# A new order for the opening of an H3 and MLP training step: v loaded in place, two filter spectra kept on chip, tap rows filled to 128

## The chip, the cores and the metric

The kernel runs on one core of a Trainium2 chip. The metric is the time of one execution in device microseconds (us), as the median of several executions. The core has five instruction queues that work side by side: TensorE (PE, matrix products; its weight loads are listed as PEld), VectorE (DVE), ScalarE (ACT), GpSimd (POOL) and SyncE (SP, which only issues transfers). POOL issues transfers too, on a queue of its own. Each queue runs its instructions strictly in the order in which they stand; an instruction whose input is not there holds up everything behind it in its queue.

## The reference

A token sequence of 2048 by 512 goes through four layers, A B A B, each of the form x = x + f(layernorm(x)); the kernel returns the output and all gradients for a given grad_out. Cut to what matters here:

```
def _A_ref(q, k, v, shift_k, ssm_k, ssm_D):          # q is layernorm(x)
    k_shift = sum over t<4 of k[:, s-t, :] * shift_k[:, t]   # short causal filter
    kv = k_shift * v
    y = irfft(rfft(pad(kv)) * rfft(pad(ssm_k)))[:S]  # long causal convolution, per column
    return q * (y + kv * ssm_D)
def _B_ref(x, w1, b1, w2, b2):                        # gelu MLP, 512 -> 1376 -> 512
    return gelu(x @ w1 + b1) @ w2 + b2
```

The long convolution does not depend on x, so kv, its spectrum, the filter's spectrum H and y are computed once, for both A layers.

## The kernel before, in words

The program has four stages: the opening, the forward convolution, the MLP with both B layers, and the backward pass. The change is in the opening and at its seam to the forward convolution.

**The opening** (function `opening`) makes, from the raw inputs, four things. First the filter: the rows of ssm_k ("hat", four loads into the memory that later holds the MLP weights, `res.w`, `w_sb` in the views) are turned by TensorE against an identity (`both`), with a reversed copy made by DVE (`hrev`), into a folded form X (`fold_x`), from which DVE makes the sums and differences `fold_s`, `fold_d`, `fold_t`. Second the sine and cosine tables `tabN` and `tabF`: POOL writes step numbers (`krow`), DVE multiplies them and masks them to a phase (`tab_u`, `tab_ph`), ACT takes the sine. Third k and v: k (`kn`) is turned into `kT`, the four-tap filter is 16 products with diagonal matrices (`wdiag`) for each of 16 token tiles (the "ks" steps, results in `ksb`), v's second half is mirrored by TensorE (the "mv" steps) and written back over v and to DRAM (`vB_d`), and DVE multiplies `ksb` by v into `kv` (`y_res` in the views). Fourth q: mirrored likewise ("mq"), its layernorm statistics taken and applied, and stored (`n_d`).

Then come 16 spectrum steps "H", in five groups `GROUPS` of 2, 2, 4, 4, 4: each is 4 or 8 matmuls of 128x512 of the folded filter with `tabN` into a PSUM tile `sp_ps`, plus one or two matmuls of 5 rows (`sp5` against `hsp`) that add five single taps, 31 of these in all. Each step is copied to SBUF (`Hg`, two slots for pairs of steps) and stored in DRAM (`Hspec_d`). Between these steps TensorE transposes the tables (steps "tt").

The order of all this is not written by hand. Each step is entered into a list (`Plan`) with an engine, an estimated duration, and what it reads and writes; `Plan.order` takes the steps by earliest start and a priority from the table `OPEN_W`; `OPEN_EV` says by a letter which engine copies each PSUM tile (A for ACT, V for DVE). The result is fixed for every queue.

**The forward convolution** (function `phase_conv_forward`) takes the five groups in turn: spectrum of kv (`spectrum`, into `KVg`), product with H on DVE (`product`: `pr_t`, `pr_u`, `Yg`), inverse transform on TensorE (`inv_group`, PSUM tile `iv_ps`). H comes from DRAM by `load_spec`, two buffers `Hg2` in rotation; groups 0 and 1 are loaded right behind the opening. Ten small matmuls (`keep_busy`, on `nyq`) stand ahead of the first inverse transform.

Of the kernel before, what the change touches and what calls it, by code (L numbers as in the profile page):

```python
# [178 lines left out]
SIN_SCALE = -(2.0 * math.pi / 8192.0) * (1.0 - SIN_EPS)  # L179
# [176 lines left out]
class InvBlocks:  # L356
# [45 lines left out]
OPEN_SLOTS = {"sp": 3, "p1": 2, "kn": 4, "hg": 2, "vt": 2, "kb": 2, "ft": 2, "ph": 2}  # L402
OPEN_EV = {"hx": "AVAAAAAV", "kt": "AAAVVAVV", "ks": "AAAAAAAAVAAAAAAA", "mv": "VAAV", "mq": "AAAA", "H": "AAAAAAAAAAAAAAVA"}
OPEN_W = {
    "PE": {1: -302, 3: 4, 4: -70, 6: 29, 7: 0},
    "ACT": {1: -63, 3: -115, 4: -256, 5: 338, 6: 142, 7: 164},
    "DVE": {1: -17, 2: -176, 3: -9, 4: 62, 5: 0, 8: 60},
    "POOL": {3: 197, 4: 117, 5: 0, 7: 78, 8: -90},
    "SP": {0: -7, 4: 29, 6: -224},
}  # L410
OPEN_FREE = {"PE": 4.2, "ACT": 3.3, "DVE": 3.8, "POOL": 8.4, "SP": 0.7}

# [4 lines left out]

def opening(nc, tc, dims, consts, dram, res, aps, tabFs, foldp, iop, hrot, gp, psum):
# [15 lines left out]
    wdiag = gp.tile([P, ND, 4, P], BF16, name="wdiag")  # L434
    krow = gp.tile([P, 1280], I32, name="krow")

# [41 lines left out]
    p = Plan(OPEN_SLOTS)  # L478
    line = {"ks": [], "H": []}

# [16 lines left out]
    def four(t):  # L497
        return t[:, :].rearrange("p (t d) -> p t d", t=4)
# [13 lines left out]
    for cc in (1, 0, 3, 2):  # L512
# [9 lines left out]
        for m in (1, 0):  # L522
            ps = ("sp", "hx", cc, m)
# [13 lines left out]
    S_(0.5, lambda b: b.nc.sync.dma_start(out=wsh, in_=aps["A_shift_k"].rearrange("(c p) j -> p c j", p=P)), 0,  # L537
       writes=[("wsh",)])
    S_(0.5, lambda b: b.nc.sync.dma_start(out=hsp[4:5, :], in_=aps["A_ssm_D"].rearrange("(o d) -> o d", o=1)), 0,
       part=[("hsp",)])  # L540

    def hs(b):
# [48 lines left out]
    def wd(b):  # L591
        for c in range(ND):
            for j in range(4):
                b.nc.vector.tensor_scalar(out=wdiag[:, c, j, :], in0=consts.ident, scalar1=wshf[:, c, j:j + 1], scalar2=None,
                                          op0=ALU.mult)
    wshf = gp.tile([P, ND, 4], F32, name="wsh_f")
    V(0.08, lambda b: b.nc.vector.tensor_copy(out=wshf, in_=wsh), 3, reads=[("wsh",)], writes=[("wshf",)])
    V(1.7, wd, 3, reads=[("wshf",)], writes=[("wd",)])
    G(0.6, lambda b: b.nc.gpsimd.dma_start(out=dram.wdiag, in_=wdiag), 3, reads=[("wd",)], kb=512.0)

# [141 lines left out]
    for g, (k1, base, n) in enumerate(GROUPS):  # L742
        key = f"h{k1}"
        for mt in range(n):
            ps, hg = ("sp", "H", g, mt), ("hg", g, mt // 2)
            need = [("tN", f, qt, int(base >= 8)) for f in range(2) for qt in range(2)] + ([("tNs", int(base >= 8))] if mt >= 2 else [])
            more = 2 if g == 0 and mt == 0 else 0

            def mm(b, g=g, mt=mt, ps=ps, key=key, k1=k1, base=base):
# [19 lines left out]
            line["H"] = [E(0.215 * (6 if k1 in (0, 4) else 10) + 0.215 * more, mm, 6, after=line["H"], writes=[ps],  # L769
                           reads=need + [("ft", key), ("sp5",), ("hsp",), ("altq",)] + ([("fd",)] if k1 == 2 else []))]  # L770
            evict(OPEN_EV["H"][base + mt], lambda b, hg=hg, mt=mt: b(hg)[:, :].rearrange("p (c m d) -> p c m d", c=2, m=2)[:, :, mt % 2, :],
                  lambda b, ps=ps: b(ps), 1, 6, reads=[ps], part=[hg])
            if mt % 2:
                S_(0.45, lambda b, hg=hg, c=base + mt - 1: b.nc.sync.dma_start(
                    out=dram.Hspec[:, :, c:c + 2, :], in_=b(hg)[:, :].rearrange("p (c m d) -> p c m d", c=2, m=2)), 6,
                   reads=[hg], kb=512.0)
# [58 lines left out]
    G(1.0, ends, 8)  # L835
    return p, tiles, stk, fk, tabI_name


@with_exitstack
def phase_conv_forward(ctx, nc, tc, dims, consts, dram, res, aps):  # L840
# [29 lines left out]
    p, tiles, stk, fk, tabI_name = opening(nc, tc, dims, consts, dram, res, aps, tabFs, foldp, iop, hrot, gp, psum)  # L870
    order = p.order(open_prio, lambda o: 0.0, dict(OPEN_FREE))
# [42 lines left out]
    for g, (k1, base, n) in enumerate(GROUPS):  # L914
# [304 lines left out]
def tok(ap2d, s):  # L1219
    return ap2d[s * 512:(s + 1) * 512, :].rearrange("(t p) d -> p t d", p=P)  # L1220
# [931 lines left out]
```

## Time and profile before

| | |
|---|---|
| median of 3 runs | 828.21 us (823.02 to 828.89) |
| the profiled execution | 826.01 us, span of its instructions 824.2 us |
| PE, DVE, ACT, POOL busy, of the span | 94%, 87%, 71%, 26% |
| opening, by the queues | about 0 to 96 us of the span |
| forward convolution, TensorE's part | about 96 to 156 us |

All times in the views count from the start of the span. Matmuls overlap in the array, so a group's busy time is longer than the distance between starts; for TensorE's pace the starts are read. A number in square brackets at the end of a timeline row is the idle time of that engine before the row, with what ended it. "issue" in the chain is time that the profile can't put down to anything. In the windows the granted TensorE clock is 1.00 for 2.4 GHz and 0.50 for 1.2 GHz. A DMA share of 1.00 means that the core's 16 DMA engines were all busy.

### The profile page before, as it was taken

The numbers are of one execution on the slowest core, as the hardware profiler recorded it, in microseconds if no ns is written. First come the engines' busy times: TensorE is split into PE (matmuls) and PEld (weight loads), VectorE is DVE, ScalarE is ACT, GpSimd is POOL, SyncE is SP. The second block draws the span as 40 slices with busy tenths as digits, with TensorE's granted clock in tenths as the row PEclk, the third lists the DMA queues.
The fourth block names the chain that finished last, engine by engine and source line by source line (L and its number), as shares of the span: only waits on it lengthen the run. The fifth ranks groups of instructions, "written<-read, shape, count | busy, mean of one in ns | idle before, by whom it ended". The sixth has DMA issues, their size and how long they took to land.

```text
span 824.2 us, 14206 instructions
## 1 busy us (share of the span) xinstructions
PE 771.1 (94%) x5312; PEld 465.6 (56%) x5312; DVE 713.4 (87%) x1273; ACT 581.9 (71%) x828; POOL 213.5 (26%) x329
## 2 busy tenths in 40 slices
PE   6889879998999999999999999998999999999997
PEld 5654334565666666667566566643444456856663
DVE  7979499898999999999889998797399999993873
ACT  5777645679999999998779966425323238797663
POOL 3725200021334343235323223330111404400000
PEclk9999979999999999999999999999999999999999
DMA  8786969524565645957858477989699999883311
GB/s 263 241 320 232 331 216 326 180 53 138 165 179 137 188 122 148 239 144 202 209 166 195 116 224 203 289 217 259 186 291 276 250 380 320 259 295 100 109 59 44
DMA packets 203211, 170.46 MB, mean 207 GB/s; under 512 B 94403, under 2 KB 180614, under 8 KB 202886
## 3 DMA queue, kind: packets, MB, share of 16 engines
q1 hardware_dynamic: 189046, 125.21, 54.3%
q0 software_dynamic: 13040, 42.25, 14.6%
q10 hardware_dynamic: 1056, 2.10, 0.7%
q8 instruction: 41, 0.67, 0.4%
q14 instruction: 28, 0.23, 0.1%
HBM read 77.41 MB, written 76.36 MB: 187 GB/s over the span
## 4 chain that ended last, share of the span: by engine, by line
PE 38%; DVE 34%; ACT 15%; issue 6%; DMA 4%; POOL 3%; ACTq 0%; SPq 0%; DVEq 0%; POOLq 0%
PE sp_ps L56 10%; ACT l_g L56 9%; DVE l_g L56 8%; PE dw_ps L56 7%; PE oo_ps L56 5%; PE mm_ps L56 4%; PE iv_ps L56 4%; PE gh_ps L56 3%; DVE Wb L56 3%; DVE l_h L56 2%; DVE b_junk L56 2%; PE p_ps L56 2%; PE gk_ps L56 2%; DVE pr_u L56 2%; PE dw_tp L56 1%
## 5 line engine op out<-in xcount | busy, mean ns | idle before, releaser
L56 ACT ACTIVATE l_g<-l_g 128x1536 bf16<-128x1536 bf16 (+1 forms) x96 | 134.4, 1431 | 1.3 <-DVE l_g L56 1.1
L56 PEld LDWEIGHTS <-l_h 128*128 128x128 bf16 x704 | 69.1, 98 | 81.5 <-DVE l_h L56 3.5
L56 PEld LDWEIGHTS <-dw_tm 128*128 128x128 bf16 x704 | 66.1, 98 | 68.3 <-ACT dw_tm L1845 0.8
L56 PEld LDWEIGHTS <-w_sb 128*128 128x128 bf16 x872 | 82.5, 98 | 34.6 <-issue 11.8
L56 PE MATMUL mm_ps<-l_nT,w_sb 128*128 128x256 bf16 x704 | 89.7, 273 | 1.0 <-ACT l_g L56 0.6
L56 PE MATMUL oo_ps<-w_sb,l_h 128*128 128x512 bf16 x352 | 82.7, 384 | 3.0 <-DVE l_h L56 2.7
L56 PE MATMUL dw_ps<-x_sl,dw_tm 128*128 128x512 bf16 x352 | 85.5, 380 | 0.0
L56 PE MATMUL dw_ps<-G,dw_tm 128*128 128x512 bf16 x352 | 84.8, 379 | 0.3 <-ACT dw_tm L1845 0.3
L56 PE MATMUL mm_ps<-l_nT,w2T_sb 128*128 128x256 bf16 x704 | 82.9, 273 | 1.3 <-ACT l_h L56 0.9
L56 PE MATMUL oo_ps<-w1T_sb,l_h 128*128 128x512 bf16 x352 | 79.1, 379 | 0.1
L56 PEld LDWEIGHTS <-w2T_sb 128*128 128x128 bf16 x704 | 68.9, 98 | 14.2 <-issue 2.1
L56 DVE TENSOR_TENSOR l_g<-l_g,l_g 128x1280 bf16<-128x1280 bf16 (+1 forms) x88 | 76.6, 883 | 0.3
L56 ACT ACTIVATE l_h<-mm_ps 128x512 bf16<-128x512 f32 (+1 forms) x96 | 51.9, 594 | 28.0 <-PE mm_ps L56 19.0
L1845 ACT ACTIVATE dw_tm<-dw_tp 128x1024 bf16<-128x1024 bf16 x44 | 44.9, 1023 | 19.9 <-PE dw_tp L56 19.5
L56 POOL TENSOR_SCALAR l_dg<-ident,b_cols 128x128 bf16<-128x128 bf16 x32 | 31.6, 987 | 75.5 <-DVE b_junk L56 72.2
L56 POOL TENSOR_SCALAR rstd<-ln_mvs 128x2 f32<-128x2 f32 x20 | 13.3, 663 | 107.3 <-DVE ln_mvs L56 107.1
L1923 ACT ACTIVATE dw_o<-dw_ps 128x512 bf16<-128x512 f32 x22 | 13.1, 595 | 38.3 <-PE dw_ps L56 29.2
L56 ACT ACTIVATE l_n<-x_sl,nmr,rstd 128x512 bf16<-128x512 bf16 x48 | 37.9, 845 | 2.8 <-POOL nmr L56 1.6
L56 ACT ACTIVATE l_g<-mm_ps,b_col 128x256 bf16<-128x256 f32 x77 | 32.6, 531 | 5.4 <-PE mm_ps L56 5.2
L56 DVE TENSOR_SCALAR l_g<-l_g 128x1536 bf16<-128x1536 bf16 (+1 forms) x64 | 32.5, 519 | 2.5 <-ACT l_g L56 2.5
L56 DVE TENSOR_REDUCE b1a<-dw_fm 128x1 f32<-128x2048 bf16 x14 | 31.5, 2278 | 1.5 <-DMA dw_fm<-gz_d 1.5
L56 ACT ACTIVATE l_n<-l_n,b_cols 128x512 bf16<-128x512 bf16 x32 | 25.4, 844 | 10.2 <-POOL b_cols L56 10.1
(316 smaller groups left out, 1656.7 us busy)
## 6 DMA issues: line engine op xcount, KB each, us to landing
h_d<-l_h SPq DMA_DIRECT2D x16, 704.0 KB
gz_d<-l_h SPq DMA_DIRECT2D x16, 704.0 KB
dw_fm<-gz_d SPq DMA_DIRECT2D x22, 512.0 KB
l_n<-n_d SPq DMA_DIRECT2D x28, 256.0 KB
n_d<-l_n SPq DMA_DIRECT2D x24, 256.0 KB
Hspec_d<-Hg SPq DMA_DIRECT2D x8, 512.0 KB
Hg<-Hspec_d SPq DMA_DIRECT2D x3, 1024.0 KB
KVspec_d<-KVg SPq DMA_DIRECT2D x3, 1024.0 KB
```

The costliest lines, as they stand in the source:

```text
L56: return self.tc.keep_in_program_order(f(*args, **kwargs))
L1845: nc.scalar.activation(out=dst, in_=ps, func=ACT.Identity)
L1923: nc.scalar.activation(out=o, in_=ps, func=ACT.Identity)
```

## The change

- **v in place.** The four loads of v go into the memory of `kv` itself. They no longer wait for a slot of `vt`. The product with `ksb` then overwrites v, so it comes after the store of v's mirrored half to `vB_d` has read it.
- **Two spectra kept.** A tile `Hkeep` holds groups 0 and 1 of H from the opening on; they are still stored for the backward pass, but no longer loaded for the forward one. Group 2 is loaded behind the opening, group 3 into `Hkeep` after the product of group 1, group 4 into the one `Hg2` that is left.
- **Tap rows filled to 128.** `hsp` and `sp5` get 128 rows of which 123 are zero (two memsets on DVE at the front), so the 31 tap matmuls have 128 rows. They, and `krow` (now 16-bit), live in unused ends of `res.w`.
- **Tap masks held back.** The two DVE masks `tap_ph` may enter the list only from 9 us of its clock on.
- The 16 multiplications that make `wdiag` become one with a broadcast operand; the letters in `OPEN_EV` move two copies of v and one of k from DVE to ACT and one of q and one of ks the other way (those of hx and H only change places); 22 instead of 20 matmuls on the identity at the start; new numbers in `OPEN_W`, and so another order on every queue.

```diff
-OPEN_EV = {"hx": "AVAAAAAV", "kt": "AAAVVAVV", "ks": "AAAAAAAAVAAAAAAA", "mv": "VAAV", "mq": "AAAA", "H": "AAAAAAAAAAAAAAVA"}
+OPEN_EV = {"hx": "AAVAAAAV", "kt": "AAAAVVAV", "ks": "AAAAAAAVAAAVAAAA", "mv": "AAAA", "mq": "AVAA", "H": "AVAAAAAAAAAAAAAA"}
 OPEN_W = {
-    "PE": {1: -302, 3: 4, 4: -70, 6: 29, 7: 0},
+    "PE": {1: -464, 3: 11, 4: 31, 6: 37, 7: 7},
...
-    krow = gp.tile([P, 1280], I32, name="krow")
+    krow = res.w.flat[0][:, 2 * S + 16:2 * S + 16 + 1280].bitcast(I16)
-    hsp = gp.tile([5, D], BF16, name="hsp")
+    hsp = res.w.centre
-    sp5 = gp.tile([5, 2, 5 * P], BF16, name="sp5")
+    sp5 = res.w.flat[1][:, 2 * S + 16:2 * S + 16 + 1280].rearrange("p (f q) -> p f q", f=2)
...
+    def zero(b):
+        b.nc.vector.memset(hsp, 0.0)
+        b.nc.vector.memset(sp5, 0.0)
+    V(0.7, zero, 1, writes=[("hsp",), ("sp5",)])
...
-        V(0.48, lambda b, u=u: ...bitwise_and), 1, writes=[nm])
+        late.add(V(0.48, lambda b, u=u: ...bitwise_and), 1, writes=[nm]))
...
     def wd(b):
-        for c in range(ND):
-            for j in range(4):
-                b.nc.vector.tensor_scalar(out=wdiag[:, c, j, :], in0=consts.ident, scalar1=wshf[:, c, j:j + 1], ...
+        b.nc.vector.tensor_tensor(out=wdiag..., in0=consts.ident[:, :].unsqueeze(1).to_broadcast([P, 4 * ND, P]),
+                                  in1=wsh[...].unsqueeze(2).to_broadcast([P, 4 * ND, P]), op=ALU.mult)
...
     for i in range(4):
-        S_(0.45, ...dma_start(out=four(b(("vt", "v", i))), in_=tok(v_ap, i)), 0, writes=[("vt", "v", i)],
-           kb=512.0, after=prods[i - 2:i - 1] if i > 1 else ())
+        S_(0.45, ...dma_start(out=kv[:, 4 * i:4 * i + 4, :], in_=tok(v_ap, i)), 0, writes=[("v", i)], kb=512.0)
...
-        prods.append(V(1.23, prod, 3, reads=[("kb", "k", i), ("vt", "v", i)], part=[("kv",)]))
+        prods.append(V(1.23, prod, 3, reads=[("kb", "k", i), ("v", i)], writes=[("v", i)], part=[("kv",)]))
...
-            ps, hg = ("sp", "H", g, mt), ("hg", g, mt // 2)
+            ps, hg = ("sp", "H", g, mt), ("hg", g, mt // 2) if g > 1 else ("hk", g)
...
+    hkeep = iop.tile([P, 2, 4, 512], BF16, name="Hkeep")
-    for _ in range(20):
+    for _ in range(22):
...
-        Hs.append(invp.tile([P, 2, 4, 512], BF16, name="Hg2", tag="Hg2", bufs=2))
+        Hs.append(hkeep if g == 3 else invp.tile([P, 2, 4, 512], BF16, name="Hg2", tag="Hg2", bufs=1))
-    load_spec(0)
-    load_spec(1)
+    Hs += [hkeep[:, :, 0:2, :], hkeep[:, :, 2:4, :]]
+    load_spec(2)
...
-        if g + 2 < 5:
+        if 1 <= g <= 2:
             load_spec(g + 2)
```

**DVE at the start of the opening** (`hrev` is the reversed filter row, `tap_ph` the mask, `tab_u` and `tab_ph` the table phases, `fold_x` a copy of a turned filter tile). Before:

```order
L56 CAST pvh<-pvh_i 128x2
L56 TENSOR_SCALAR tap_ph<-tap_ph 5x640 x2
L56 COPY hrev<-w_sb 128x1024
L56 MEMSET hrev 128x4
L56 TENSOR_SCALAR tab_u<-krow,pvn 128x768
```

and now:

```order
L56 CAST pvh<-pvh_i 128x2
L56 MEMSET w_centre 128x256
L56 MEMSET w_sb 128x640
L56 COPY hrev<-w_sb 128x1024
L56 MEMSET hrev 128x4
L56 TENSOR_SCALAR tab_u<-w_sb,pvn 128x768
```

The two masks have left the place ahead of the first reversed row (they now stand behind the third and the fourth), and two memsets that wait for nothing have taken it.

**SP at the seam** (stores of H and of the normalized q, then the loads of H and the stores of kv's spectrum). Before:

```order
L56 DMA Hspec_d<-Hg_181 256x1x1024
L56 DMA n_d<-w_sb 128x4x512 x3
L56 DMA Hspec_d<-Hg_180 256x1x1024
L56 DMA Hg_1285<-Hspec_d 128x2x1024
L56 DMA Hg_1287<-Hspec_d 128x2x1024
L56 DMA KVspec_d<-KVg 256x1x1024
```

and now:

```order
L56 DMA n_d<-w_sb 128x4x512 x2
L56 DMA Hspec_d<-Hg_180 256x1x1024
L56 DMA n_d<-w_sb 128x4x512
L56 DMA Hg_1270<-Hspec_d 128x2x2048
L56 DMA KVspec_d<-KVg 256x1x1024 x2
```

The two loads of groups 0 and 1 behind the last store are gone; in their place stands one load, of group 2, and the last store of q now comes after the last store of H.

**POOL in the middle of the opening** (`ks_d` and `kT_d` are stores for the backward pass, `vB_d` and `qB_d` those of the mirrored halves). Before:

```order
L56 DMA qB_d<-w_sb 128x2x512
L56 DMA vB_d<-vt_182 128x2x512
L56 DMA qB_d<-w_sb 128x2x512 x3
L56 DMA vB_d<-vt_183 128x2x512
L56 DMA ks_d<-ksb_185 128x2048
L56 COPY kT<-kT 128x4x3
L56 DMA kT_d<-kT 128x8704
L56 DMA vB_d<-vt_182 128x2x512
```

and now:

```order
L56 DMA vB_d<-y_res 128x2x512
L56 COPY kT<-kT 128x4x3
L56 DMA vB_d<-y_res 128x2x512
L56 DMA kT_d<-kT 128x8704
L56 DMA ks_d<-ksb_185 128x2048
L56 DMA vB_d<-y_res 128x2x512 x2
```

All four stores of v now come ahead of those of q; the last two stand behind the store of `kT`, and each of them has to be through before DVE's product may overwrite that part of v.

## Rows read from the trace of the kernel before

**Rows 1.** Windows: stretch, length, busy PE, PEld, DVE, ACT, POOL, clock, DMA share.
```profile
8.20:94.00 85.80, 78.54 (x673) 46.79 (x674) 75.15 (x145) 63.44 (x78) 37.47 (x49) 0.98 0.77 272
```
**Rows 2.** The chain of waits at the seam: start us, us, what.
```profile
95.62 8.55 DMA Hg<-Hspec_d
...
105.45 0.17 DVE pr_t L56
...
107.95 0.61 DVE Yg L56
...
108.61 3.57 PE iv_ps L56 x8
```
**Rows 3.** Timeline of ACT at the seam: start us, us, row.
```profile
96.93 2.86 ACT L296 ACTIVATE KVg<-sp_ps 128x1024 bf16<-128x1024 f32 x3 [0.19 <-PE sp_ps L56]
```
**Rows 4.** Timeline of PE at the seam and in the forward convolution.
```profile
98.46 1.25 PE L56 MATMUL iv_ps<-nyq,ident 128*128 128x256 bf16 x10
108.61 1.86 PE L56 MATMUL iv_ps<-Yg,vt 128*128 128x512 bf16 x4 [8.89 <-DVE Yg L56]
...
119.22 1.03 PE L56 MATMUL iv_ps<-Yg,vt 128*128 128x512 bf16 x4
120.08 1.03 PE L56 MATMUL iv_ps<-Yg,ksb 128*128 128x512 bf16 x4
```
**Rows 5.** Windows at the seam, columns as in the first group.
```profile
104.00:106.00 2.00, 0.00 (x0) 0.00 (x0) 1.60 (x5) 0.00 (x0) 0.00 (x0) 0.50 0.91 351
```
**Rows 6.** Timeline of DVE at the start.
```profile
6.26 0.72 DVE L56 TENSOR_SCALAR tap_ph<-tap_ph 5x640 int32<-5x640 int32 x1 [2.11 <-POOL tap_ph L471]
7.68 0.64 DVE L56 TENSOR_SCALAR tap_ph<-tap_ph 5x640 int32<-5x640 int32 x1 [0.69 <-POOL tap_ph L471]
8.24 0.40 DVE L56 COPY hrev<-w_sb 128x1024 bf16<-128x1024 bf16 x1
8.69 0.62 DVE L56 TENSOR_SCALAR tab_u<-krow,pvn 128x768 int32<-128x768 int32 x1
```
**Rows 7.** Timeline of PE at the start.
```profile
4.47 0.39 PE L56 MATMUL sp_ps<-both,w_sb 128*128 128x256 bf16 x1 [0.36 <-DMA w_sb<-in_A_ssm_k_dram]
8.71 0.40 PE L56 MATMUL sp_ps<-both,hrev 128*128 128x256 bf16 x1 [3.84 <-DVE hrev L56]
```
**Rows 8.** Timeline of PE in one H step of ten matmuls.
```profile
69.64 0.39 PE L56 MATMUL sp_ps<-hsp,sp 5*128 5x512 bf16 x1
69.96 1.04 PE L56 MATMUL sp_ps<-fold_t,tabN 128*128 128x512 bf16 x4
70.93 0.39 PE L56 MATMUL sp_ps<-hsp,sp 5*128 5x512 bf16 x1
```
**Rows 9.** Groups of PE by shape, 38.7 to 94.2: busy us, mean ns.
```profile
L56 PE MATMUL sp_ps<-fold_t,tabN 128*128 128x512 bf16 x88 | 24.3, 381 | 0.0
L56 PE MATMUL sp_ps<-hsp,sp 5*128 5x512 bf16 x31 | 11.9, 385 | 0.0
```
**Rows 10.** Who waited for whom, PE, 8.7 to 96: us, times, longest.
```profile
PE sp_ps L56 <- DMA vt<-in_A_v_dram: 2.4, 1, 2.4
PE p_ps L56 <- ACT ksb L56: 1.4, 2, 0.7
PE sp_ps L56 <- DVE kT L56: 1.3, 1, 1.3
```
**Rows 11.** Timeline of DVE: the diagonals, a copy from PSUM, a memset.
```profile
18.09 2.69 DVE L56 TENSOR_SCALAR wdiag<-ident,wsh_f 128x128 bf16<-128x128 bf16 x16
...
53.73 1.23 DVE L56 CAST vt<-sp_ps 128x1024 bf16<-128x1024 f32 x1 [2.69 <-PE sp_ps L56]
...
126.81 0.48 DVE L56 MEMSET w_centre<- 128x512 bf16 x1 [0.17 <-DVE w_sb L56]
```
**Rows 12.** Issues of transfers before 96: count, KB each, us to landing.
```profile
kT_d<-kT POOLq DMA_DIRECT2D x1, 2176.0 KB, 9.2
...
vB_d<-vt POOLq DMA_DIRECT2D x4, 256.0 KB, 3.5
```

More of the change, by code (lines that the diff above doesn't have):

```diff
@@ L402, with opening @@
 OPEN_SLOTS = {"sp": 3, "p1": 2, "kn": 4, "hg": 2, "vt": 2, "kb": 2, "ft": 2, "ph": 2}
-OPEN_EV = {"hx": "AVAAAAAV", "kt": "AAAVVAVV", "ks": "AAAAAAAAVAAAAAAA", "mv": "VAAV", "mq": "AAAA", "H": "AAAAAAAAAAAAAAVA"}
+OPEN_EV = {"hx": "AAVAAAAV", "kt": "AAAAVVAV", "ks": "AAAAAAAVAAAVAAAA", "mv": "AAAA", "mq": "AVAA", "H": "AVAAAAAAAAAAAAAA"}
+OPEN_FREE = {"PE": 4.4, "ACT": 3.3, "DVE": 4.2, "POOL": 9.0, "SP": 0.7}
 OPEN_W = {
-    "PE": {1: -302, 3: 4, 4: -70, 6: 29, 7: 0},
[L406 to L409, printed above, removed]
+    "PE": {1: -464, 3: 11, 4: 31, 6: 37, 7: 7},
+    "ACT": {1: -441, 3: -237, 4: -358, 5: 436, 6: 201, 7: 70},
+    "DVE": {1: -333, 2: -77, 3: 151, 4: 332, 5: 112, 8: -88},
+    "POOL": {3: 335, 4: -45, 5: 22, 7: -90, 8: -305},
+    "SP": {0: 126, 4: -128, 6: -90},
 }
-OPEN_FREE = {"PE": 4.2, "ACT": 3.3, "DVE": 3.8, "POOL": 8.4, "SP": 0.7}
 def open_prio(o):
     return OPEN_W.get(o.eng, {}).get(o.stage, 0) - o.up
-def opening(nc, tc, dims, consts, dram, res, aps, tabFs, foldp, iop, hrot, gp, psum):
+def opening(nc, tc, dims, consts, dram, res, aps, tabFs, foldp, iop, hrot, gp, psum, hkeep):
     S, D, NT, ND = dims.S, dims.D, dims.NT, dims.ND
@@ L478, in opening @@
     p = Plan(OPEN_SLOTS)
-    line = {"ks": [], "H": []}
+    line, late = {"ks": [], "H": []}, set()
     def adder(eng, lat0):
@@ L538, in opening @@
        writes=[("wsh",)])
+    def zero(b):
+        b.nc.vector.memset(hsp, 0.0)
+        b.nc.vector.memset(sp5, 0.0)
+    V(0.7, zero, 1, writes=[("hsp",), ("sp5",)])
     S_(0.5, lambda b: b.nc.sync.dma_start(out=hsp[4:5, :], in_=aps["A_ssm_D"].rearrange("(o d) -> o d", o=1)), 0,
-       part=[("hsp",)])
+       reads=[("hsp",)], part=[("hspD",)])
     def hs(b):
@@ L548, in opening @@
     E(0.3, hs, 1, reads=[("hat", cc) for cc in range(4)], writes=[("p1", "hs")])
-    V(0.68, lambda b: b.nc.vector.tensor_copy(out=hsp[0:4, :], in_=b(("p1", "hs"))[0:4, :]), 1, reads=[("p1", "hs")],
-      part=[("hsp",)])
+    V(0.68, lambda b: b.nc.vector.tensor_copy(out=hsp[0:4, :], in_=b(("p1", "hs"))[0:4, :]), 1, reads=[("p1", "hs"), ("hsp",)],
+      part=[("hspD",)])
     for f, u in enumerate((sp5u, krow5)):
         nm = ("five", f)
-        V(0.48, lambda b, u=u: b.nc.vector.tensor_single_scalar(out=u, in_=u, scalar=8191, op=ALU.bitwise_and), 1, writes=[nm])
+        late.add(V(0.48, lambda b, u=u: b.nc.vector.tensor_single_scalar(out=u, in_=u, scalar=8191, op=ALU.bitwise_and), 1, writes=[nm]))
         def five(b, f=f, u=u):
-            b.nc.scalar.activation(out=sp5[:, f, :], in_=u, func=ACT.Sin, scale=SIN_SCALE, bias=consts.pibias[0:5, :])
-        A(0.81, five, 1, reads=[nm], part=[("sp5",)])
+            b.nc.scalar.activation(out=sp5[0:5, f, :], in_=u, func=ACT.Sin, scale=SIN_SCALE, bias=consts.pibias[0:5, :])
+        A(0.81, five, 1, reads=[nm, ("sp5",)], part=[("sp5r",)])
     def small(b):
-        b.nc.vector.memset(sp5[:, 1, 0:1], 1.0)
+        b.nc.vector.memset(sp5[0:5, 1, 0:1], 1.0)
         b.nc.vector.memset(altq, 0.0)
         b.nc.vector.tensor_copy(out=altq[:, 0:1], in_=consts.alt)
-    V(0.3, small, 1, writes=[("sp5",), ("altq",)])
+    V(0.3, small, 1, writes=[("sp5r",), ("altq",)])
     fold = Fold(nc, foldp, True)
@@ L569, in sums @@
         fold.open(hld["X"])
-    V(2.29, sums, 2, reads=[("hX",), ("sp5",)], writes=[("fs",)])
+    V(2.29, sums, 2, reads=[("hX",), ("sp5r",)], writes=[("fs",)])
     def stream(k1, key, dur, **kw):
@@ L591, in wd @@
     def wd(b):
-        for c in range(ND):
-            for j in range(4):
[L594 to L598, printed above, removed]
+        b.nc.vector.tensor_tensor(out=wdiag[:, :, :, :].rearrange("p c j q -> p (c j) q"),
+                                  in0=consts.ident[:, :].unsqueeze(1).to_broadcast([P, 4 * ND, P]),
+                                  in1=wsh[:, :, :].rearrange("p c j -> p (c j)").unsqueeze(2).to_broadcast([P, 4 * ND, P]), op=ALU.mult)
+    V(2.28, wd, 3, reads=[("wsh",)], writes=[("wd",)])
     G(0.6, lambda b: b.nc.gpsimd.dma_start(out=dram.wdiag, in_=wdiag), 3, reads=[("wd",)], kb=512.0)
@@ L768, in mm @@
                         b.nc.tensor.matmul(psb[:, h, :], lhsT=a, rhs=r, start=(i == 0), stop=(i == len(lst) - 1))
[L769 to L771 removed]
+            line["H"] = [E(0.05 + 0.215 * (6 if k1 in (0, 4) else 10) + 0.215 * more, mm, 6, after=line["H"], writes=[ps],
+                           reads=need + [("ft", key), ("sp5r",), ("hspD",), ("altq",)] + ([("fd",)] if k1 == 2 else []))]
+            evict(OPEN_EV["H"][base + mt], lambda b, spec=spec, mt=mt: spec(b)[:, :, mt % 2, :],
                   lambda b, ps=ps: b(ps), 1, 6, reads=[ps], part=[hg])
             if mt % 2:
[L774 to L775 removed]
+                S_(0.45, lambda b, spec=spec, c=base + mt - 1: b.nc.sync.dma_start(out=dram.Hspec[:, :, c:c + 2, :], in_=spec(b)), 6,
                    reads=[hg], kb=512.0)
@@ L791, in ev @@
             b.nc.scalar.activation(out=dst(b), in_=b(ps).bitcast(BF16).rearrange("p (k q) -> p k q", k=8), func=ACT.Identity)
-        E(0.46, mm, stage, reads=reads, writes=[ps], after=after)
+        E(0.5, mm, stage, reads=reads, writes=[ps], after=after)
         A(1.02, ev, stage, reads=[ps], part=[nm])
@@ L835, in opening @@
     G(1.0, ends, 8)
-    return p, tiles, stk, fk, tabI_name
+    return p, tiles, stk, fk, tabI_name, lambda o: 9.0 if o in late else 0.0
 @with_exitstack
```

14 lines of the change are left out of this document (8 added, 6 removed).

## The prediction, made before the changed kernel was run

> **What bounds the kernel now.** I read the windows first, for how full each queue is; then the chain of waits and the timelines where it crosses from the opening into the forward convolution; then the timelines of DVE and TensorE at the start and around one H step; last the list of waits. In the opening two queues are nearly full: of 85.8 us TensorE is busy 78.5, DVE 75.2, so DVE is idle for 10.65; ACT is busy 63.4 and the transfers 77% [rows 1]. So an edit pays there only as far as both TensorE and DVE come forward. At the seam nothing is full. The last store of H, then the load of group 0 back from DRAM (8.55 us), then DVE's product, then the inverse transform follow each other [rows 2], and TensorE idles 8.89 us [rows 4]. kv's spectrum of group 0 was copied out at about 97.9 (the second of three copies that begin at 96.93 and take 2.86 together) [rows 3], so from there to the product at 105.45 [rows 2] the load alone holds things up. Behind the seam TensorE sets the time until about 156, and then stages follow that begin when the one before ends: I carry whatever the seam wins to the end, one for one.
>
> **The change part by part.** The sum is made against the profiled execution, 826.0 us; the median of the runs is 828.2, 2.2 above it.
>
> *Start.* TensorE has its first filter row at 4.47 but waits until 8.71 for the reversed copy [rows 7], because DVE stands 2.11 and 0.69 us in front of masks whose input POOL has not made [rows 6]. Free of them, DVE is ready at 6.26 - 2.11 = 4.15. Now the memsets come first: one as the row of 0.48 us, one with 2.5 times its columns, so 0.5 to 1.2 [rows 11]. The copy then starts at 5.1 to 5.9 in place of 8.24: 2.3 to 3.1 us, I take 2.7, nearer to the middle as the second memset's pace is unknown. The masks (1.36) are still paid by DVE, later, behind work that TensorE then has. Next to be late is ACT's sine of them, which only the H steps need.
>
> *Tap rows.* A tap matmul with 5 rows lasts 385 ns against 381 with 128 [rows 9], but what counts is the distance of the starts. 69.64 to 69.96 is 0.32 for the tap; the next tap starts 0.97 after that, for four matmuls [rows 8], where four at full pace take 120.08 - 119.22 = 0.86 [rows 4]. So a tap takes 0.32 - 0.215 + 0.97 - 0.86 = 0.21 us more than an ordinary matmul, 31 times [rows 9]: 6.5 us, all on TensorE's full stretch. With 128 rows it is shaped like its neighbours, whose starts lie 0.215 apart; I take the whole, with nothing as the other end.
> The Trainium skill ("TensorE: Matmul & The Clock Gate", the table under "Why this matters for your kernels") says that a single matmul with K=32 takes the same time as one with K=128. By that sentence the filling wins nothing; the row on the length of one agrees with it, the starts do not.
>
> *v.* TensorE waits 2.4 us for the third load of v, which waited for its slot [rows 10], DVE 2.69 behind it [rows 11]. Without the slot the four loads go out behind those of k, in the first third of the opening. I take 2.4.
>
> *Other waits of TensorE.* 1.4 on copies by ACT, 1.3 on one of kT, and some like them [rows 10]. A new order moves such waits more than it removes them. Between nothing and 4, I take 2.
>
> So TensorE: 2.7 + 6.5 + 2.4 + 2.0 = 13.6 us.
>
> *DVE.* It starts 2.7 earlier, and its work changes: two copies of v and one of k leave, one of q and half a one come (1.23 each [rows 11]): -1.8. One multiplication of 2048 columns takes the place of 16 that took 2.69 [rows 11]: between 0.8 (twice the 0.40 of a copy of 1024 [rows 6]) and 2.5 (twice the slow 1.23), I take 2.3, since its second operand is not read in steps of one: -0.4. The 16-bit `krow` has the same number of elements (0.62 us for 768 [rows 6]); I price it at nothing, with up to 1.2 ns per element as the other end, 2 us on all six. The memsets lie in the start term, and of the masks 1.36 come in. Without any wait, DVE could therefore end its part 10.65 + 2.7 + 1.8 + 0.4 - 1.36 = 14.2 us earlier. ACT gains two and a half copies of about a microsecond on 63 in 86 [rows 1], and stays third.
>
> *Both together.* 13.6 and 14.2 are floors of the same size; two queues that feed each other don't both run without a wait. Of DVE's 10.65 idle, 2.69 is the wait for v; I leave some 4.4 us of the other 8 in the new order. The opening then gets 13.6 - 4.4 = 9.2 us shorter.
>
> *The reload.* With groups 0 and 1 on chip the product waits for kv's spectrum, not for the load: 105.45 - 97.9 = 7.5 us. Next to be late is the DVE work ahead of it, which is why I count it after the allowance above. Group 2 is loaded behind the last store of q; at the 8.55 of today's load [rows 2] it is covered, as group 1's product and three folds stand ahead of its use.
>
> *The clock.* TensorE idles from 99.7 to 108.6 [rows 4], by 104 the granted clock is 0.50 [rows 5], and the first eight matmuls take 3.57 us [rows 2] where eight at full pace take 1.73: 1.8 lost. With 7.5 us less idle, 1.4 is left for the clock to fall in. Between nothing and 1.8, I take 1.3.
>
> *At no price:* v's product in place (its stores: last rival), the extra store order on SP, two more matmuls at the start, which TensorE does while it waits for the first row.
>
> Sum: 9.2 + 7.5 + 1.3 = 18.0; 826.0 - 18.0 = **808 us**.
>
> **The rivals.**
> *Tap matmuls keep their distance.* The cause of the 0.32 may be the change of operand and not the rows; against that, TensorE goes from one table to another at its full pace elsewhere [rows 4]. Then TensorE wins 7.1, it alone is the bound, and 3 us of waits stay: 4.1 + 7.5 + 1.3 = 13; 813 us. The skill's sentence above would give this one. 0.12.
> *The transfers become the bound.* 77% of 85.8 us is 66 us [rows 1]; pressed into some 74 that is 90%, and landings get late: the two H slots, q, group 2 of H. If the opening wins only 3 us for it: 3 + 7.5 + 1.3 = 12; 814 us. For it: the 8.55 for 512 KB at the seam. Against: nearly all that is moved there is stores, for which no engine waits. 0.12.
> *DVE's tail.* Two of the four q are mirrored only near the end, and their statistics, POOL's root and the scaling stand in DVE's queue ahead of the first product. If the product waits for them as long as it won by the reload, only 9.2 + 1.3 stay: 815.5 us. 0.07.
> *Slower: v's product waits for its stores.* DVE may overwrite v only when `vB_d` has read it. Such a store takes 3.5 us, and the last two now stand behind `kT_d`, which takes 9.2 [rows 12]. If none of it were covered, two products would wait 3.5 and two 12.7, 32 us in DVE's queue, with all of H's copies behind them: 826 - 18 + 32 = 840 us. It decides if DVE comes to a product within those times of the copy of v; above 18 us in sum it turns the gain. Against: the loads of v no longer wait for a slot, so its copies and stores come early, too. 0.04.
> *The change does not do what it says* where the product still waits at the seam, for group 2's load or a tile whose memory a store still reads: the reload term falls to 1 or 2, 814 us. 0.03.
>
> **How the numbers follow.** The forecast has 0.62: its own range goes from all terms at their good end and no allowance beyond 1 us (DVE's 14.2 less 1: 826 - 13.2 - 7.5 - 1.8 = 803.5) to 814 with 6 more of waits. The rivals at 813 to 815.5 have 0.34 and lie inside or just beyond; the runs before spread from 5 below the median to 1 above, which widens both ends by some 3 us. Range: 800 to 818. About 1% is what a measurement of this kernel can tell from no change: faster means below 819.9. Faster 0.91, within 1% 0.06 (two of the middle rivals together, or v's stores in part), slower 0.03.
>
> **What would show it.** In the changed kernel's profile: the first reversed copy before 6; tap matmuls 0.215 from start to start; no PE wait on a load of v; no load of H in the chain at the seam, the product within about 1 us of the copy of kv's spectrum or of DVE's own last fold; the first inverse matmuls at the full pace; the product near 89, the inverse transform near 92. I am wrong if DVE shows waits on `vB_d`, if PE's idle time on ACT and DVE in the opening goes above 10 us, or if the stages behind 156 don't come forward with the seam.

## The result, and the profile after

The changed kernel takes **802.07 us** (median, 801.39 to 803.57) against 827.37 for the kernel before, run beside it: a ratio of 0.9705 [0.9665, 0.9745]. The profiled execution takes 801.39 us, its span 799.5; before it was 826.01. So 24.6 us are gone where 18.0 were forecast. Nearly all of it is gone by the seam: DVE's first product came forward from 105.45 [rows 2] to 82.76, 22.7 us. The forward convolution adds 0.6, the stages up to the last work of DVE 0.4, and from the start of that last row of DVE to the end of the span it is 1.0 less. This last 1.0 can't be put down to the change: that stretch takes 7.5 us in this trace and 8.2 to 9.4 in all the others, that of the kernel before and those of the variants below.

Windows of the opening, to 85 us (columns as in [rows 1], which had PE 78.54 and DVE 75.15 in a stretch 6.3 us longer):

```profile
5.50:85.00 79.50, 74.99 (x693) 51.08 (x703) 76.74 (x136) 69.86 (x85) 35.42 (x65) 1.00 0.91 328
```

The list of waits, DVE and then PE, 5 to 96 and 5 to 85 us (us in total, times, longest):

```profile
DVE w_centre L56 <- PE p_ps L56: 0.9, 1, 0.9
DVE pr_t L56 <- ACT KVg L296: 0.4, 1, 0.4
...
PE sp_ps L56 <- ACT Hg L56: 1.2, 1, 1.2
PE sp_ps L56 <- ACT fold_x L56: 1.0, 4, 0.3
PE sp_ps L56 <- DVE hrev L56: 0.7, 1, 0.7
```

These two lists are the heart of it. DVE, idle for 10.65 us before, is idle for 2.76 in this window (79.50 - 76.74). Of these, 1.3 are listed waits, and none is on a store of v. TensorE shows no wait on a load of v [rows 10]. The transfers rose to 91%, and the one listed wait of PE or DVE on a transfer is 0.3 us, on a filter row.

The chain at the seam (start us, us, what), where [rows 2] had a load of 8.55 us:

```profile
78.60 1.03 ACT Hg L56
...
80.79 0.84 ACT KVg L296
...
81.71 1.03 ACT KVg L296
...
86.46 2.21 DVE fold_d L56
```

PE there, answering [rows 4]: the wait for Yg is 1.51 instead of 8.89, and the first matmuls of the inverse run near their full pace, but then TensorE waits for DVE's fold.

```profile
85.91 1.20 PE L56 MATMUL iv_ps<-Yg,vt 128*128 128x512 bf16 x4 [1.51 <-DVE Yg L56]
86.94 1.02 PE L56 MATMUL iv_ps<-Yg,ksb 128*128 128x512 bf16 x4
88.72 0.39 PE L56 MATMUL sp_ps<-fold_d,tabF 128*128 128x512 bf16 x1 [0.75 <-DVE fold_d L56]
```

DVE, for [rows 6, 11]: the memsets, the first reversed row, the table phase from the 16-bit `krow` (listed as w_sb), a mask, the diagonals in one piece.

```profile
3.73 0.27 DVE L56 MEMSET w_centre<- 128x256 uint32 x1
4.08 0.59 DVE L56 MEMSET w_sb<- 128x640 uint32 x1
4.59 0.90 DVE L56 COPY hrev<-w_sb 128x1024 bf16<-128x1024 bf16 x1
...
9.01 0.61 DVE L56 TENSOR_SCALAR tab_u<-w_sb,pvn 128x768 int32<-128x768 int16 x1
...
10.60 0.47 DVE L56 TENSOR_SCALAR tap_ph<-tap_ph 5x640 int32<-5x640 int32 x1
...
16.18 2.29 DVE L56 TENSOR_TENSOR wdiag<-ident,wsh 128x2048 bf16<-128x2048 bf16 x1
```

PE at its first reversed row and in an H step, for [rows 7, 8]: 5.68 instead of 8.71, and the tap (`w_centre,w_sb`) starts 0.22 before what follows it instead of 0.32.

```profile
5.68 0.39 PE L56 MATMUL sp_ps<-both,hrev 128*128 128x256 bf16 x1 [0.68 <-DVE hrev L56]
...
71.39 0.38 PE L56 MATMUL sp_ps<-w_centre,w_sb 128*128 128x512 bf16 x1
71.61 1.03 PE L56 MATMUL sp_ps<-fold_t,tabN 128*128 128x512 bf16 x4
72.47 0.38 PE L56 MATMUL sp_ps<-w_centre,w_sb 128*128 128x512 bf16 x1
```

### The profile page after: what moved, and what is told of

Read it like the earlier page. It is cut to its first block, busy times and chain, and to the rows that moved or that the text cites. A ratio compares the mean times of both kernels' runs of the same rounds, so it can differ in the third digit from the quotient of the medians.

```text
span 799.5 us, 14109 instructions
## 1 busy us (share of the span) xinstructions
PE 755.8 (95%) x5236; PEld 466.4 (58%) x5314; DVE 711.5 (89%) x1258; ACT 581.4 (73%) x829; POOL 208.3 (26%) x329
## 4 chain that ended last, share of the span: by engine, by line
PE 35%; DVE 30%; ACT 18%; issue 9%; DMA 4%; POOL 2%; ACTq 0%; DVEq 0%; POOLq 0%
ACT l_g L56 10%; PE sp_ps L56 8%; DVE l_g L56 6%; PE oo_ps L56 6%; PE dw_ps L56 5%; PE mm_ps L56 4%; PE gh_ps L56 3%; PE iv_ps L56 3%; DVE Wb L56 3%; ACT l_n L56 2%; DVE l_h L56 2%; PE p_ps L56 2%; DMA Hb<-Hspec_d 2%; DVE b_junk L56 2%; DVE pr_u L56 2%
## 5 line engine op out<-in xcount | busy, mean ns | idle before, releaser
L56 PEld LDWEIGHTS <-w_sb 128*128 128x128 bf16 x903 | 86.0, 99 | 40.3 <-issue 13.6
L56 PE MATMUL dw_ps<-x_sl,dw_tm 128*128 128x512 bf16 x342 | 83.3, 379 | 0.6
L56 PE MATMUL oo_ps<-w_sb,l_h 128*128 128x512 bf16 x341 | 80.1, 379 | 3.7 <-DVE l_h L56 2.9
L56 PE MATMUL dw_ps<-G,dw_tm 128*128 128x512 bf16 x338 | 82.6, 379 | 0.9 <-ACT dw_tm L1851 0.3
L56 PE MATMUL oo_ps<-w1T_sb,l_h 128*128 128x512 bf16 x339 | 77.2, 379 | 0.8
```

The costliest lines, as they stand in the source:

```text
L56: return self.tc.keep_in_program_order(f(*args, **kwargs))
```

## The experiments

My theory: the opening has two full queues, TensorE and DVE, and what is taken off or put on either one moves the seam nearly one for one; the reload (the load of H back from DRAM at the seam) is a piece of its own behind it. The rivals: the edits on one queue win nothing (the tap rows, the start, v), or the new order, not the edits, made the gain. The measure is the start of the first product (`pr_t` of group 0) in the span, since it is the same place in each run; the change has 82.76. It comes from one profiled execution of each variant and can move by some tenths by itself: ahead of the place where the variant "wdiag twice" differs from the change, one wait of DVE was 0.2 us in its trace and 0.9 in that of the change. The intervals of the adjacent taps, of the masks placed first and of the three wdiag variants overlap that of the change, so there the reading rests on the seam.

| variant | median us | ratio to before [95%] | first product, against the change |
|---|---|---|---|
| the change | 802.07 | 0.9705 [0.9665, 0.9745] | 82.76 |
| taps of 5 rows | 809.63 | 0.9796 [0.9759, 0.9833] | 88.50, +5.7 |
| taps of 5 rows, adjacent | 805.86 | 0.9746 [0.971, 0.9781] | 85.61, +2.9 |
| taps of 64 rows | 809.89 | 0.9801 [0.9762, 0.9839] | 88.73, +6.0 |
| groups 0 and 1 loaded again | 811.85 | 0.9818 [0.9796, 0.9841] | 90.79, +8.0 |
| tables of numbers of before | 812.08 | 0.9825 [0.9802, 0.9848] | 90.71, +8.0 |
| masks not held back | 810.99 | 0.9793 [0.9768, 0.9818] | 88.58, +5.8 |
| v in slots | 809.0 | 0.979 [0.9765, 0.9815] | 84.28, +1.5 |
| wdiag twice on DVE | 804.63 | 0.972 [0.9703, 0.9737] | 84.40, +1.6 |
| masks first, order kept | 806.84 | 0.975 [0.9728, 0.9771] | 85.06, +2.3 |
| wdiag on POOL | 804.89 | 0.972 [0.9698, 0.9743] | 83.42, +0.7 |
| wdiag on POOL, 4 pieces | 802.33 | 0.9689 [0.9652, 0.9725] | 82.06, -0.7 |
| kernel before, taps of 128 rows | 823.75 | 0.9959 [0.9931, 0.9986] | 102.21, -3.2 against before |

**The rows of the taps.** Three variants of the change, order kept.

```diff
-    R.append((sp5[:, 0, g * P:(g + 1) * P], hsp))
+    R.append((sp5[0:5, 0, g * P:(g + 1) * P], hsp[0:5, :]))
...
```

The line of the second tap, `Z`, gets the same `0:5`.

> The changed kernel with one thing undone: the 31 tap matmuls read 5 rows again instead of 128; order and all else as in the change. My theory (a tap with 5 rows stands 0.21 us further apart than an ordinary matmul, on a TensorE stretch with nearly no idle time): 31 x 0.21 = 6.5 us more, so 807 to 809 instead of 802.1, ten-matmul steps 2.56 us instead of 2.16. Rival (the length of one matmul does not depend on its rows, so the filling wins nothing): 802 within 1.5.

The second variant reads 5 rows too, and puts the second tap of a step first in its sum, next to the first one:

```diff
-    Z.append((sp5[:, 1, g * P:(g + 1) * P], hsp))
+    Z.insert(0, (sp5[0:5, 1, g * P:(g + 1) * P], hsp[0:5, :]))
```

> As the run with 5-row taps, but in steps with two taps they stand next to each other (the first one last in its sum, the second one first in its sum). If the price is that of going from 128 rows to 5 and back, it is paid once per pair: 16 times instead of 31, about 3.3 us more than the changed kernel, 805 to 806. If each 5-row matmul costs 0.21 us by itself, wherever it stands: 807 to 809, as with taps apart.

The third has `0:64` where the first has `0:5`.

> The changed kernel with tap matmuls of 64 rows (59 of them zero) instead of 128. If any row count other than that of the neighbours brings the 0.21 us: 807 to 809, as with 5 rows. If the price depends on how few the rows are: something between 802 and 805, with starts between 0.215 and 0.32 apart.

PE in one H step, with 5 rows, with 5 rows adjacent, and with 64:

```profile
65.72 0.38 PE L56 MATMUL sp_ps<-w_centre,w_sb 5*128 5x512 bf16 x1
66.03 1.04 PE L56 MATMUL sp_ps<-fold_t,tabN 128*128 128x512 bf16 x4
67.00 0.38 PE L56 MATMUL sp_ps<-w_centre,w_sb 5*128 5x512 bf16 x1
```

```profile
65.81 1.03 PE L56 MATMUL sp_ps<-fold_t,tabN 128*128 128x512 bf16 x4
66.77 0.60 PE L56 MATMUL sp_ps<-w_centre,w_sb 5*128 5x512 bf16 x2
67.31 1.04 PE L56 MATMUL sp_ps<-fold_t,tabN 128*128 128x512 bf16 x4
```

```profile
65.93 0.39 PE L56 MATMUL sp_ps<-w_centre,w_sb 64*128 64x512 bf16 x1
66.25 1.04 PE L56 MATMUL sp_ps<-fold_t,tabN 128*128 128x512 bf16 x4
67.22 0.39 PE L56 MATMUL sp_ps<-w_centre,w_sb 64*128 64x512 bf16 x1
```

A lone tap of 5 rows: 0.31 to the next start, and 0.97 for the four after it, 0.1 more than in the stream each time, so 0.2 a tap and 6.4 in all. The adjacent pair: 0.54 for two, 0.96 for the four ahead of it, 0.2 for the pair, so half. With 64 rows the distances are those of 5. So it is not the few rows that cost, and not each such matmul; it is each entry from 128 rows into 5 or 64 and each return, about 0.1 us apiece. Row counts between 64 and 128 were not tried. The rival, that filling the rows wins nothing, is refuted. The length of one tap is the same in all of them (0.38 to 0.39), so the sentence of the Trainium skill on single matmuls that I weighed in the prediction stands; it just does not price a stream. A rule that may bear on it stands on another page: the Trainium skill ("TensorEngine Tiling (Array Packing)", "Tiling Modes", under "Key Properties") says that changing the tiling mode drains TensorE. A price per change and not per matmul is what that would give, and the runs agree. That a plain matmul of 5 or 64 rows is such a change of mode neither that section nor a run here shows.

**The taps alone, in the kernel before.** `hsp` and `sp5` filled to 128 rows, two memsets ahead of the opening, nothing else.

```diff
-    hsp = gp.tile([5, D], BF16, name="hsp")
+    hsp = gp.tile([P, D], BF16, name="hsp")
+    nc.vector.memset(hsp, 0.0)
...
```

> The kernel before with one part of the change alone: taps filled to 128 rows in tiles of their own (two memsets ahead of the opening's list), order and all else as before. If TensorE's stretch is the bound there too: 31 x 0.21 = 6.5 us less, 820.5 to 822.5 against 827.4. If the old order's waits (DVE idle 10.65 us) take back what TensorE wins: 825 to 827. At the start the memsets may add up to 0.7 us, as TensorE waits for DVE there.

The time is between the two. The last four-matmul piece of H starts at 87.80 instead of 92.44, 4.6 of the 6.4 earlier; of the rest the wait for v, 3.5 instead of 2.4, took 1.1, and 0.7 was not followed up. Then the chain has the load again:

```profile
90.86 10.08 DMA Hg<-Hspec_d
...
102.21 0.17 DVE pr_t L56
...
105.37 3.57 PE iv_ps L56 x8
```

It begins 4.8 earlier and takes 1.5 longer than in [rows 2]. Alone, the taps win 3.2 at the seam; a little over half of what they are worth in the new order.

**The reload.** Ahead of the load of group 2:

```diff
+    for g in range(2):
+        nc.sync.dma_start(out=Hs[g], in_=dram.Hspec[:, :, 2 * g:2 * g + 2, :])
```

> The changed kernel, but groups 0 and 1 of H are loaded again from DRAM into the kept tile at the seam (two loads on SP's queue ahead of that of group 2, behind the last stores). Theory (the load held up the product in the kernel before): the product of group 0 waits for it, 6 to 8 us later than 82.8 in the span, and the first inverse matmuls fall to half the clock, 0 to 1.8 more: 808 to 812. Rival (what the change won at the seam came from the new order, and a load fits beside the work there): 802 within 1.5.

As the theory has it: the chain goes over the load, and the eight matmuls are back at 3.57.

```profile
81.67 7.91 DMA Hkeep<-Hspec_d
89.60 0.31 DVE spec_rb L56
...
90.79 0.17 DVE pr_t L56
...
93.94 3.57 PE iv_ps L56 x8
```

The product is 8.03 later, the end of the forward convolution 8.7, the whole 9.8.

**The order.** The changed code with the numbers of before in `OPEN_EV`, `OPEN_FREE` and `OPEN_W`.

```diff
-    "PE": {1: -464, 3: 11, 4: 31, 6: 37, 7: 7},
+    "PE": {1: -302, 3: 4, 4: -70, 6: 29, 7: 0},
...
```

> The changed code with the numbers of the kernel before in the tables that set the order and the copying engines of the opening (the masks still held back, v in place, taps of 128 rows, spectra kept). Theory (the 6 us won beyond my forecast came from the order, which took out nearly all waits between TensorE and DVE): 3 to 8 us more, 805 to 810, with DVE idle 4 us or more in the opening. Rival (the edits themselves give it all, the table nothing): 802 within 1.5.

The time, 10.0 more, is 2 us beyond the upper end of the theory. DVE now starts with two table steps, and the first reversed row comes at 7.26 instead of 4.59. DVE's waits, 5 to 90:

```profile
DVE y_res L56 <- ACT ksb L56: 2.5, 1, 2.5
DVE hrev L56 <- DMA w_sb<-in_A_ssm_k_dram: 0.9, 1, 0.9
DVE w_centre L56 <- PE p_ps L56: 0.5, 1, 0.5
```

With a wait of 0.2 that makes 4.1. Then the product waits 3.35 for KVg, since TensorE is late too: its first reversed row comes 2.1 later (7.79), and the granted clock is 0.50 again for a stretch, at 44 to 46 us. So the same code, with numbers that don't fit it, has more than the waits that I had left in. Even so its product is 14.7 ahead of that of the kernel before: of the 22.7 at the seam, some 8 need the new order, and the edits win the rest without it.

**Masks not held back, and v in slots.** In both, the numbers of the change meet a list that they were not made for, so order and edit change together.

```diff
-    return ..., lambda o: 9.0 if o in late else 0.0
+    return ..., lambda o: 0.0
```

> The changed kernel without the bound that holds the two tap masks back; the planner puts them where it likes. Theory: they stand ahead of the first reversed copy again, wait there for POOL, and TensorE starts 2.5 to 3 us later, all of which reaches the end: 804.5 to 805. Rival (a late start is made up in the opening, since the start is not on a full stretch): 802 within 1.

My theory of the place was wrong: the masks came behind the first reversed row (TensorE starts at 5.68 as in the change) and ahead of the second. DVE waits 1.8 us for POOL there, and TensorE's listed waits up to the product sum to 7.0 instead of 4.3 in the change.

```diff
-    S_(0.45, ...dma_start(out=kv[:, 4 * i:4 * i + 4, :], ...), 0, writes=[("v", i)], kb=512.0)
+    S_(0.45, ...dma_start(out=four(b(("vt", "v", i))), ...), 0, writes=[("vt", "v", i)], kb=512.0,
+       after=prods[i - 2:i - 1] if i > 1 else ())
...
```

> The changed kernel with v loaded into the rotating slots again, each later load only when a product has freed one; the planner's numbers as in the change. Theory: one load of v is late again and TensorE waits about 2.4 us for it: 804 to 805. Rival (in the new order the slots come free in time, so that v in place wins nothing): 802 within 1.

No wait on a load of v came back; the seam is 1.5 later by small waits. Some 2.2 more arise behind it, in the forward convolution, where ACT's copy of KVg waits 6.65 for a store (chain):

```profile
84.28 14.05 DMA KVspec_d<-KVg
```

That trace is of the slowest of the six executions (814.23, median 809.0), so what it shows behind the seam need not hold for the others. How much of the gain belongs to v alone, these two don't tell.

**The start, by itself.** The order of the change, only the two masks moved ahead of the first reversed row.

```diff
+    masks = [o for o in order if o in p.masks]
+    order = [o for o in order if o not in p.masks]
+    at = order.index(p.rev[0])
+    order[at:at] = masks
...
```

> The changed kernel with the two tap masks placed right ahead of the first reversed row on DVE, every other step in the order of the change. POOL has the second mask's input at about 8.5 us of the span, so the first reversed row comes 4 us later. If the start counts one for one: the product near 87 instead of 82.8, time about 806. Rival (a late start is made up further on): the product within 1 of 82.8, time 802 to 803.

```profile
6.33 0.73 DVE L56 TENSOR_SCALAR tap_ph<-tap_ph 5x640 int32<-5x640 int32 x1 [1.66 <-POOL tap_ph L473]
7.75 0.64 DVE L56 TENSOR_SCALAR tap_ph<-tap_ph 5x640 int32<-5x640 int32 x1 [0.69 <-POOL tap_ph L473]
8.32 0.40 DVE L56 COPY hrev<-w_sb 128x1024 bf16<-128x1024 bf16 x1
```

POOL was ready sooner than I had reckoned: TensorE's first reversed row is 3.25 later (8.93), not 4. The product is 2.30 later, so the rival is refuted: a late start is not made up. The difference is 0.95, and the masks that DVE need not do later take 2 x 0.47. That would be one for one, but other rows moved too: the first copy took 0.40 where it took 0.90 in the change, and a table phase (`tab_ph`) 0.56 instead of 1.04. So what is shown is that some 70% of this late start reaches the seam.

**DVE's slack.** The multiplication of wdiag done twice (`for _ in range(2):` around it).

> The changed kernel with the one multiplication that makes wdiag done twice, one behind the other in DVE's queue: 2.29 us more of DVE at 16 us of the span, order and all else as in the change. If DVE has no slack in the changed opening (it idles about 1.3 us up to the seam): the product of group 0 comes 1.5 to 2.3 us later than 82.8, time 803.5 to 804.5. Rival (TensorE alone sets the opening and DVE's queue has room): the product within 0.5 of 82.8, time within 1 of 802.

The product came 1.64 later for 2.29. The 0.65 is DVE's wait for `p_ps` at 13 us, which was 0.2 instead of 0.9 in this run; it stands ahead of the edit, so it is no slack that the edit used up. The multiplication itself reaches the seam whole. This run does not tell through which queue: TensorE, too, waited 1.7 us for `wdiag`.

**Less work for DVE.** The same multiplication on POOL, in one piece and in four.

```diff
-        b.nc.vector.tensor_tensor(out=wdiag[:, :, :, :].rearrange("p c j q -> p (c j) q"),
+        b.nc.gpsimd.tensor_tensor(out=wdiag[:, :, :, :].rearrange("p c j q -> p (c j) q"),
```

> The changed kernel with the multiplication that makes wdiag issued on POOL instead of DVE, in the same place of the order: 2.29 us less of DVE, on POOL it falls into an idle stretch of 9 us. If DVE alone bounds the opening: the product 1.5 to 2.3 earlier, 800 or a little less. If TensorE stands as close behind (31 rows of taps already moved the seam by 5.7 for 6.5 of TensorE): the product 0 to 0.5 earlier, 801.5 to 802. If POOL's multiplication ends later than the 18.96 at which TensorE first reads wdiag: slower by that much.

None of the three. POOL was done at 15.03, long before TensorE's first use, and yet the product came 0.7 later (the time is 2.8 up; of the rest see the end of the next section). DVE's second mask shows where the 2.29 went (POOL's row of 11 us, then DVE's):

```profile
11.23 3.80 POOL L56 TENSOR_TENSOR wdiag<-ident,wsh 128x2048 bf16<-128x2048 bf16 x1 [1.86 <-DMA wsh<-in_A_shift_k_dram]
...
11.61 3.76 DVE L56 TENSOR_SCALAR tap_ph<-tap_ph 5x640 int32<-5x640 int32 x1
```

3.76 us instead of 0.47: it began while POOL's instruction ran, and ended 0.34 after it. (In that run the first filter row also landed about 0.8 later than in the change, of which 0.15 was left by DVE's first mask, 10.75 instead of 10.60.)

> As the run with wdiag on POOL, in which one of DVE's masks of 5x640 took 3.76 us instead of 0.47 and ended together with POOL's multiplication of 3.80 us; here POOL makes wdiag in four pieces of 512 columns. If DVE is held until the one POOL instruction that runs has ended: a DVE instruction is held for about 1 us at most, DVE keeps most of its 2.29, and the product comes 0 to 1 us earlier than 82.8 (802 or a little less). If DVE is held until POOL has no more of such work: as in one piece, some 3.3 us on a DVE row, the product 0.5 to 1 later, 803 to 805.

```profile
11.45 1.20 DVE L56 TENSOR_SCALAR tap_ph<-tap_ph 5x640 int32<-5x640 int32 x1
...
14.59 1.46 DVE L56 TENSOR_SCALAR tab_ph<-tab_ph 128x768 int16<-128x768 int16 x2
```

The first of the two: a hold lasts as long as one POOL instruction, not as long as POOL has work. DVE comes to `fold_s`, the row behind, 0.76 earlier (17.62 instead of 18.38), and the product is 0.7 earlier, with TensorE's first use of `wdiag` where it was (18.98, before 18.96). So what DVE won came out at the seam nearly whole. The product then waits 0.82 for KVg instead of 0.40, so TensorE's side stands right behind. The time, 802.33, is that of the change.

## Why the prediction was right, and where it was short

The side and the mechanism were right: two full queues, a reload in series behind them, and the later stages coming forward with the seam. (One for one it was in the change; variants lost more behind the seam, see below.) The measured 802.07 lies in the range near its fast end; the point, 808, was 6 too slow. By its own steps:

- *Start*, 2.7: 3.03 measured (8.71 to 5.68). This is near by two errors against each other. The two memsets overlap and end at 4.67, so the copy starts at 4.59, 3.65 earlier and below my lower bound; but it takes 0.90 instead of 0.40. That most of the start counts at the seam is shown by the masks placed first.
- *Tap rows*, 6.5: 6.4 by the distances, 5.7 at the seam when undone. The rival that they "keep their distance" (0.12) did not come true: with 128 rows the starts are 0.22 apart, though the operands change as before.
- *v*, 2.4: the wait is gone, but undoing it brought 1.5 at the seam with no wait on v, so the term is not shown on its own.
- *Other waits of TensorE*, 2.0: copies by ACT and DVE held it 5.0 in before and 3.3 now, 1.7 less. What I had not seen is a stretch of half clock in the middle of the old opening, behind idle times of 1.34 and 1.35 us; it is not in the change. It lasts some 3.4 us, so by an estimate from its length up to 1.7 us were lost in it (windows of the kernel before, columns as in [rows 1]):

```profile
31.00:32.00 1.00, 1.00 (x10) 0.89 (x9) 1.00 (x3) 0.65 (x1) 0.36 (x1) 0.50 0.85 328
32.00:33.00 1.00, 1.00 (x11) 0.96 (x10) 1.00 (x1) 0.37 (x1) 0.37 (x2) 0.50 0.49 193
33.00:34.00 1.00, 1.00 (x7) 0.48 (x5) 0.97 (x3) 0.69 (x2) 1.00 (x2) 0.50 0.11 41
```

- *DVE's work*: wdiag 2.29 for the 2.3 taken, the 16-bit `krow` at 0.61 for 0.62, so nothing for it. Right.
- *Both together*, the step that failed: "I leave some 4.4 us of the other 8 in the new order." KVg of group 0 was copied at 82.7 instead of 97.9, so TensorE's side of the opening is 15.2 shorter, not 9.2. The 6.0 between is nearly the whole error: 4.4 is the allowance, and 1.6 is what TensorE won beyond the 13.6 of its terms, mostly the half clock above. The allowance was a guess put where the order was there to be read: with the numbers of before the same code is 8.0 later at the seam. So it fits an order that is not tuned to its list, and this one was. The sum also took both floors to end at the same place. DVE's last fold of the opening ended at 93.9 in the kernel before, 4 us ahead of KVg, and ends at 81.4 now: DVE won only 12.5 of its 14.2, and that was enough (DVE, before and after):

```profile
91.56 2.35 DVE L56 TENSOR_TENSOR fold_t<-fold_s 128x2048 bf16<-128x2048 bf16 x2
```

```profile
80.15 1.22 DVE L56 TENSOR_TENSOR fold_t<-fold_s 128x2048 bf16<-128x2048 bf16 x1
```

- *The reload*, 7.5: 105.45 - 82.76 - 15.2 = 7.5, and 8.0 when put back. The 97.9 is the end of the first of the three copies in [rows 3], not of the second; group 0's other copy stands ahead of them. The number holds.
- *The clock*, 1.3: the granted clock stays at 1.00, and the eight matmuls take 2.1 instead of 3.57, which is 1.5; but then TensorE waits 0.75 for `fold_d` on DVE, so 0.6 is left at the end of the forward convolution.
- *The slower rival*: DVE waited for no `vB_d`. *The transfers as the bound*: 91% in the opening, as reckoned, and 0.3 us of listed waits on them.

The terms are not a sum of independent gains: the undoings at the seam (5.7, 8.0, 5.8, 1.5, and 8.0 for the tables) are more than the 22.7 that all of it won, since each disturbs one order.

**Behind the seam**: undone taps cost 5.7 at the seam but 7.6 in the time. In that profile the other 1.9 arises at about 545, in the backward pass, whose queues are the same in both. It is not a longer wait: TensorE's waits for the table `tabFb` there are 0.95 and 1.90, against 0.78 and 1.89 in the change. But behind them the granted clock fell to 0.50 (1.2 GHz), where it stayed at 1.00 in the change, and the eight matmuls from 545.02 on took 3.4 us instead of 1.7. With 5 rows, then the change (a PE row, and a window with columns as in [rows 1]):

```profile
544.77 0.46 PE L56 MATMUL sp_ps<-fold_d,tabFb 128*128 128x512 bf16 x1 [1.90 <-DMA tabFb<-tabF_d]
546.00:548.00 2.00, 2.00 (x6) 0.63 (x5) 0.00 (x0) 0.00 (x0) 0.00 (x0) 0.50 1.14 257
```

```profile
538.83 0.39 PE L56 MATMUL sp_ps<-fold_d,tabFb 128*128 128x512 bf16 x1 [1.89 <-DMA tabFb<-tabF_d]
540.00:542.00 2.00, 2.00 (x11) 0.89 (x10) 0.00 (x0) 1.02 (x1) 0.00 (x0) 1.00 1.18 251
```

So the same work with nearly the same waits can lose 1.7 us to the clock in one execution and nothing in another. Five other variants (64 rows, old tables, masks not held back, v in slots, wdiag on POOL in one piece) lose 2.5 to 7.5 us behind the forward convolution in their profiled execution. Longer waits on loads of H, KV and `n_d` are among them, and so are windows of half clock at 655 to 670 in three of them (64 rows, v in slots, wdiag on POOL). Two of these executions (64 rows, v in slots) lie 4 and 5 us above the median of their variant.

**Open**: what makes those loads later, and which part of those losses is there in every execution, wasn't tried.

## What to carry to other kernels

Where two queues are full and feed each other, find both, and the next wait of each, before you price an edit on one. Work taken off TensorE alone won 3.2 of 6.4 us in the old order, where other waits grew; in the tuned order the same work put back cost 5.7, and 0.76 taken off DVE won 0.70. Where the order of each queue is known, walk the two lists with durations from rows, instead of leaving an allowance for waits; an order fitted to its list had almost none, the same code with other numbers lost 8 us at the seam. And read a matmul's price from the distance of the starts: a few matmuls of 5 or 64 rows in a stream of 128 rows cost at every change, so fill them up or put them side by side. Last, judge an edit of one stage at the end of that stage: behind it, executions differ by as much as such an edit wins.

## What the runs showed of the hardware

- In a stream of matmuls of 128 rows, entering and leaving one of fewer rows costs about 0.1 us each way, with 5 rows as with 64 (0.31 and 0.32 to the next start instead of 0.22, 0.97 for the four ahead instead of 0.86); two of 5 rows next to each other pay it once (0.54 for both).
- A DVE instruction can be held for the whole of a POOL instruction: 3.76 us instead of 0.47, and 1.20 when POOL's work was cut in four. DVE's copies from PSUM were not held (1.20 at 12.58 in the four-piece run, while POOL worked). The Trainium skill ("SBUF — State Buffer", "Who interferes with whom") says that a DVE instruction in one of the modes that use two ports contends with GpSimd: the one that issues first has the shared ports for its whole instruction, and the other blocks. The trace agrees in the length of the hold. That this mask runs in such a mode, no run shows. So moving work to an idle POOL has a price on DVE: here 3.29 us of hold for 2.29 us moved.
- After nearly the same waits (0.95, 0.25 and 1.90 us; 0.78, 0.25 and 1.89) the granted clock fell to 0.50 in one execution and stayed at 1.00 in another; where it fell, the starts of matmuls of 512 columns lay 0.43 us apart instead of 0.22.
